# One ScalarE instruction per weight tile is tied to its place in the written order, and the stash tiles' decode starts six units after the load

## The chip, the cores and the metric

The kernel runs on one core of one Trainium2 chip, in one launch. The metric is device time in microseconds (us) from the first to the last instruction and what lies around them, as the median of several runs; less is better. The engines are TensorE (PE in the profile, its weight loads PEld), VectorE (DVE), ScalarE (ACT), GpSimd (POOL) and SyncE (SP), which issues every DMA of this kernel.

## The reference, cut to what matters

The weights arrive as 64-bit words on the device (where the host gives double precision), and the kernel turns each into float32 and then into a pair of float16, high and low; products of pairs are summed in float32. What is computed, for 8 batches of 576 tokens and 512 channels:

```python
kv = einsum('bhsd,bhse->bhde', k, v); o = einsum('bhsd,bhde->bhse', q, kv)
x = o / sqrt(mean(o*o, -1) + 1e-6) * g_norm          # heads side by side: 512 channels
theta = x @ w_theta
y = einsum('ts,bsd->btd', w_tok_r, x*cos(theta)) + einsum('ts,bsd->btd', w_tok_i, x*sin(theta))
u = x + y
x2 = u + relu(u @ w_ch)
u2 = x2 + (relu(x2.T @ w_tok1) @ w_tok2).T
out = u2 + relu(u2 @ w_ch1) @ w_ch2                  # 512 -> 1536 -> 512
```

## The kernel before

The kernel goes through the batches one after another, and then through eight large stages of the last two products (`mlp`), 64 us each. In the batch part each batch is made of small **units of work**, python generators with a `yield` between their steps. `go(unit)` first moves every pending unit on by one step and then starts the new one, so a step that stands behind n yields is written n units after the start of its own unit. The units of a batch from the third on, in this order: eight `mix` (27 matmuls each, into `py`), eight `channel` (12 matmuls, `pr`), `kv`, four `token1` (`ph`), `kv`, eight `token2` (`pu`); between them the next batch's five `attend` (`po`) and five `rotate` (`pt`) are put in. That makes 45 units with the five weight tiles below.

`spare()` puts units of weight preparation from the list `extra` in between. Beside the `channel` units of the first batch these are eleven tiles of `w_tok1` and `w_tok2` (`weight`: load, one yield, decode). From then on they are 24 tiles of `w_ch1` and `w_ch2` (`stash`, tiles `wa` and `wb` in the profile): each is loaded into `raw`, decoded, combined on GpSimd, split into `hi` and `lo`, and stored to device memory for `mlp`. Two stash tiles start in a batch's `widen_tokens` (behind its first and its fifth `token2`) and, from the third batch on, three more in its `mix` stage (behind `mix` 0, 2 and 5). The text calls the five that follow one another in this way S1 to S5. There are four batches with all five, then S1 and S2 alone once more; the batch ahead of them has two as well.

A stash tile has these steps: load on SP (L194 by way of L116); ScalarE's first decode step (L122); three VectorE steps (L124, L126, L127), the last two of which write into `raw`; four GpSimd instructions (L205 to L208) and ScalarE's L209; VectorE's L211; ScalarE's L213; VectorE's L215; two stores on SP (L218). `raw`, `hi`, `lo` and `t` have two buffers each. The other steps that matter: `mix` adds its sum to R on VectorE (L422), ScalarE writes `uh` (L423) and VectorE `ul` (L426); `channel` reads `uh` and `ul` on TensorE, and then runs L446 (VectorE), L447 (ScalarE), L453 (VectorE) and a transposing DMA into `xt` (L457), which `token1` waits for. `attend` goes through L298, L300 to L303, L308, L321, L323, a transposing DMA (L324), L327 and L329; `rotate` starts on ScalarE with L352. `kv` ends with ScalarE's L273.

Each engine executes its own queue in order. What that order is, the framework's scheduler decides when the program is built: of the instructions that it takes to be ready it issues the one written first, by its own estimate of when things finish. An instruction can therefore be queued far ahead of its written place when its engine has nothing else to do by that estimate. `tc.keep_in_program_order(x)` puts `x` behind the instruction of the same engine that was written just before it. Before the change it stands only at the loads (L116), for SP's queue.

Of the kernel before, what the change touches and what calls it, by code (L numbers as in the profile page):

```python
# [11 lines left out]
F32 = mybir.dt.float32  # L12
I32 = mybir.dt.int32
AF = mybir.ActivationFunctionType
# [14 lines left out]
def attn_mixer_kernel(  # L29
# [4 lines left out]
    nc = tc.nc  # L34
# [79 lines left out]
    def load(dst, src):  # L114

        tc.keep_in_program_order(nc.sync.dma_start(dst, src))  # L116

    def decode(val, raw, inplace=False):


        bits = val.bitcast(I32)
        nc.scalar.activation(val, raw[..., 1].bitcast(F32), AF.Copy, scale=2.0**-112)  # L122
        yield
        nc.vector.tensor_scalar(bits, bits, 3, None, ALU.logical_shift_left)  # L124
        to = raw[..., 0] if inplace else bits
        nc.vector.scalar_tensor_tensor(to, raw[..., 0], 29, bits, ALU.logical_shift_right, ALU.bitwise_or)  # L126
        nc.vector.scalar_tensor_tensor(to, raw[..., 1], -(2**31), to, ALU.bitwise_and, ALU.bitwise_or)  # L127

    def weight(pool, w, row, col, part, n, hi, lo, scale, name, raw=None):

        val = pool.tile([P, n], F32, tag="val", name=f"{name}v")[:part]
        rows = slice(row, row + part)
        if w.dtype == F32:
            load(val, w[rows, col:col + n])
            yield
        else:
            if raw is None:
                raw = pool.tile([P, n, 2], I32, tag="raw", name=f"{name}r")[:part]
                load(raw.rearrange("p n w -> p (n w)"), w.bitcast(I32)[rows, 2 * col:2 * (col + n)])
            yield  # L140
            yield from decode(val, raw)
        if w is not w_theta and w is not w_ch1:

            nc.scalar.activation(val, val, AF.Copy, scale=scale)
            nc.scalar.activation(hi, val, AF.Copy)
            yield
            nc.gpsimd.tensor_tensor(lo, val, hi, ALU.subtract)
            return
        nc.scalar.activation(hi, val, AF.Copy, scale=scale)
        yield  # L150
        nc.vector.scalar_tensor_tensor(lo, val, scale, hi, ALU.mult, ALU.subtract)
# [25 lines left out]
    wad = [dr.tile([P, KH, DH, 7, P], F16, name=f"wad{i}") for i in range(2)]  # L177
    wbd = [dr.tile([P, KH, MH, 7, P], F16, name=f"wbd{i}") for i in range(2)]

    wp = []  # L180

    def stash(w, name, rows, cols, dst):


        hi, lo = (wp[0].tile([P, 7, P], F16, tag=f"st{i}", name=f"{name}{i}") for i in range(2))

        words = () if w.dtype == F32 else (2,)
        raw = wp[0].tile([P, 4, P, *words], I32 if words else F32, tag="raw", name=f"{name}r")
        t = wp[0].tile([P, 4, P], F32, tag="val", name=f"{name}s")
        for half, at in ((0, slice(0, 4, 3)), (1, slice(1, 3))):  # L190
            src = (w.bitcast(I32) if words else w)[rows[half]:rows[half] + P, :]
            n = 2 if words else 1
            src = src.rearrange("p (a n) -> p a n", a=2)[:, :, n * cols:n * (cols + P)]
            load(raw[:, at].rearrange("p a n w -> p a (n w)") if words else raw[:, at], src)  # L194

        for _ in range(4):
            yield
        val = raw
        if words:

            yield from decode(t.rearrange("p x n -> p (x n)"), raw.rearrange("p x n w -> p (x n) w"), True)
            val = raw[..., 0].bitcast(F32)
        yield

        nc.gpsimd.tensor_tensor(t[:, 1], val[:, 3], val[:, 2], ALU.add)  # L205
        nc.gpsimd.tensor_tensor(t[:, 3], val[:, 3], val[:, 0], ALU.subtract)
        nc.gpsimd.tensor_tensor(t[:, 2], t[:, 1], val[:, 0], ALU.subtract)
        nc.gpsimd.tensor_tensor(t[:, 0], val[:, 1], t[:, 2], ALU.subtract)  # L208
        nc.scalar.activation(hi[:, :3], val[:, :3], AF.Copy, scale=SW)  # L209
        yield  # L210
        nc.vector.scalar_tensor_tensor(lo[:, :3], val[:, :3], SW, hi[:, :3], ALU.mult, ALU.subtract)  # L211
        yield
        nc.scalar.activation(hi[:, 3:], t, AF.Copy, scale=SW)  # L213
        yield
        nc.vector.scalar_tensor_tensor(lo[:, 3:], t, SW, hi[:, 3:], ALU.mult, ALU.subtract)  # L215
        yield
        for d, src in zip(dst, (hi, lo)):
            nc.sync.dma_start(d, src)  # L218

    def stash_wide(g, k):  # L220
        return stash(w_ch1, f"wa{g}{k}_", (k * P, (DH + k) * P), g * P, [t[:, g, k] for t in wad])

    def stash_narrow(g, m):
        return stash(w_ch2, f"wb{g}{m}_", (g * P, (KH + g) * P), m * P, [t[:, g, m] for t in wbd])
# [472 lines left out]
    tk, cp, first = [], [], iter(())  # L697
# [40 lines left out]
    for b in range(B):  # L738
# [49 lines left out]
        elif b + 2 == B:  # L788
# [11 lines left out]
            first = chunks(0)  # L800
# [59 lines left out]
```

## Time and profile before

| | us |
|---|---|
| median of 3 runs | 1177.6 (1174.95 to 1178.34) |
| the profiled execution | 1177.31 |
| its span, first to last instruction | 1175.5 |
| TensorE busy in the span | 1089.8 (93%) |
| VectorE busy | 849.6 (72%) |
| ScalarE busy | 562.5 (48%) |
| GpSimd busy | 236.3 (20%) |

The batch part takes the first 740 us, of which the stash tiles occupy 157 to about 560; `mlp` takes the rest. In the rows a time is in us from the start of the span; "idle before" is how long the engine stood still ahead of an instruction, and behind the arrow stands what ended that.

### The profile page before, as it was taken

The page shows a single profiled execution, that of the slowest core. Times are in us where ns is not written, and L with a number is a line of the kernel's source. Part 1 is how long each engine was busy: PE and PEld are TensorE (multiplying, and loading weights), DVE is VectorE, ACT ScalarE, POOL GpSimd, SP SyncE. Part 2 cuts the span into 40 slices and gives each one's busy share as a digit, 9 for nine tenths or more (in the row PEclk, how much of TensorE's full clock was granted, in tenths as well). Part 3 has the DMA queues.
Part 4 walks back from the last instruction along what each step waited for, and adds up shares of the span by engine and source line. Part 5 has one row for each costly group of instructions (what it writes and reads, how often), then busy time and mean ns, then how long its engine had stood idle before and what let it go on. Part 6 is the DMA issues. An engine that isn't in the chain of part 4 may idle for free.

```text
span 1175.5 us, 21915 instructions
## 1 busy us (share of the span) xinstructions
PE 1089.8 (93%) x8884; PEld 820.7 (70%) x8884; DVE 849.6 (72%) x1579; ACT 562.5 (48%) x1002; POOL 236.3 (20%) x258
## 2 busy tenths in 40 slices
PE   4759899898997997989999999999999999999998
PEld 3446666576665765767686777777777777777777
DVE  3997869798597696895955386857768584848583
ACT  2765645455264363462633163545536272626361
POOL 3774135072351450722400000000000000000000
PEclk9779999999998999999999999999999999999999
DMA  9616464592674666736273540101020202011101
GB/s 321 214 59 135 98 208 115 150 230 68 195 175 106 191 156 156 199 86 166 61 195 100 166 168 31 52 26 56 11 71 11 72 4 78 2 42 40 37 6 41
DMA packets 156357, 126.37 MB, mean 107 GB/s; under 512 B 93216, under 2 KB 137120, under 8 KB 156256
## 3 DMA queue, kind: packets, MB, share of 16 engines
q1 hardware_dynamic: 156256, 124.98, 38.0%
q8 instruction: 69, 1.13, 0.4%
q14 instruction: 32, 0.26, 0.1%
HBM read 74.29 MB, written 29.88 MB: 89 GB/s over the span
## 4 chain that ended last, share of the span: by engine, by line
PE 39%; DVE 36%; DMA 13%; ACT 4%; POOL 3%; issue 3%; SPq 2%; DVEq 0%; ACTq 0%; POOLq 0%
DMA xt<-xs 4%; PE na L82 3%; PE na L84 3%; PE na L83 3%; DVE gl L553 3%; DVE zl L367 3%; DVE gl L601 2%; DMA c<-u2d 2%; PE pa L82 2%; ACT gh L552 2%; PE pa L83 2%; PE pa L84 2%; PE pr L83 2%; DMA wa_r<-in_w_ch 1%; PE pr L84 1%
## 5 line engine op out<-in xcount | busy, mean ns | idle before, releaser
L82 PE MATMUL py<-wmh,zh 128*128 128x256 f16 (+1 forms) x576 | 166.8, 290 | 8.6 <-DMA zh<-zt 4.8
L83 PE MATMUL py<-wml,zh 128*128 128x256 f16 (+1 forms) x576 | 166.6, 290 | 0.0
L84 PE MATMUL py<-wmh,zl 128*128 128x320 f16 (+1 forms) x512 | 147.7, 289 | 5.3 <-DVE zl L367 5.3
L82 PE MATMUL na<-gh,wbh 128*128 128x288 f16 x384 | 106.7, 286 | 9.6 <-DVE c L612 9.6
L83 PE MATMUL pa<-o,wah 128*128 128x288 f16 x384 | 109.4, 286 | 0.0
L83 PE MATMUL na<-gl,wbh 128*128 128x288 f16 x384 | 109.1, 286 | 0.0
L84 PE MATMUL na<-gh,wbl 128*128 128x288 f16 x384 | 109.0, 286 | 0.0
L82 PE MATMUL pa<-o,wah 128*128 128x288 f16 x384 | 108.6, 286 | 0.2 <-DVE pre L595 0.2
L84 PE MATMUL pa<-o,wal 128*128 128x288 f16 x384 | 108.5, 286 | 0.0
L612 DVE SCALAR_TENSOR_TENSOR c<-na,c 128x288 f32<-128x288 f32 x64 | 28.5, 456 | 79.9 <-PE na L84 79.9
L82 PE MATMUL pr<-uh,wch 128*128 128x256 f16 (+1 forms) x256 | 76.3, 298 | 9.7 <-ACT uh L423 9.6
L83 PEld LDWEIGHTS <-wbh 128*128 128x128 f16 x672 | 65.7, 98 | 27.1 <-issue 10.7
L553 DVE TENSOR_TENSOR gl<-sum,gh 128x1152 f16<-128x1152 f32 x48 | 65.1, 1356 | 24.3 <-ACT gh L552 23.4
L83 PE MATMUL pr<-ul,wch 128*128 128x256 f16 (+1 forms) x256 | 76.2, 298 | 5.5 <-DVE ul L426 5.5
L83 PEld LDWEIGHTS <-wah 128*128 128x128 f16 x672 | 65.7, 98 | 17.7 <-issue 1.1
L82 PEld LDWEIGHTS <-wah 128*128 128x128 f16 x672 | 65.7, 98 | 16.6
L82 PEld LDWEIGHTS <-wbh 128*128 128x128 f16 x672 | 65.7, 98 | 16.6
L84 PEld LDWEIGHTS <-wbl 128*128 128x128 f16 x672 | 65.7, 98 | 16.6
L84 PEld LDWEIGHTS <-wal 128*128 128x128 f16 x672 | 65.7, 98 | 16.6
L84 PE MATMUL pr<-uh,wcl 128*128 128x256 f16 (+1 forms) x256 | 76.2, 298 | 0.0
L82 PEld LDWEIGHTS <-zh 128*128 128x128 f16 x576 | 57.1, 99 | 26.0 <-DMA zh<-zt 5.4
L302 POOL TENSOR_TENSOR ri<-ss,mhalf 128x8 f32<-128x8 f32 x40 | 71.4, 1785 | 2.0
(315 smaller groups left out, 2980.9 us busy)
## 6 DMA issues: line engine op xcount, KB each, us to landing
q<-in_q SPq DMA_DIRECT2D x8, 1152.0 KB, 7.2
c<-u2d SPq DMA_DIRECT2D x32, 288.0 KB, 4.4
out<-c SPq DMA_DIRECT2D x64, 144.0 KB, 1.8
k<-in_k SPq DMA_DIRECT2D x24, 256.0 KB, 4.8
v<-in_v SPq DMA_DIRECT2D x24, 256.0 KB, 5.1
wa_r<-in_w_ch SPq DMA_DIRECT2D x24, 256.0 KB, 3.9
wb_r<-in_w_ch SPq DMA_DIRECT2D x24, 256.0 KB, 3.8
wad<-wa SPq DMA_DIRECT2D x24, 224.0 KB, 2.1
```

The source lines that it names most:

```text
L82: nc.tensor.matmul(acc, ah, bh, start=first and i == 0, stop=False, **more)
L83: nc.tensor.matmul(acc, ah, bl, start=False, stop=False, **more)
L84: nc.tensor.matmul(acc, al, bh, start=False, stop=last and i == n - 1, **more)
L302: nc.gpsimd.tensor_tensor(ri, ss, mhalf, ALU.pow)
L367: nc.vector.tensor_tensor(zl[:, kk, :], t, zh[:, kk, :], ALU.subtract)
L552: nc.scalar.activation(h.hi[:, 3:], h.s, AF.Copy)
L553: nc.vector.tensor_tensor(h.lo[:, 3:], h.s, h.hi[:, 3:], ALU.subtract)
L601: nc.vector.tensor_tensor(h.lo[:, :3], h.own, h.hi[:, :3], ALU.subtract)
L612: nc.vector.scalar_tensor_tensor(dst, acc, 1.0 / SW**2, dst, ALU.mult, ALU.add)
```

## The change

The list `wp` is declared earlier, so that `decode` can ask whether the pool for the later weight tiles is open. If it is, ScalarE's first decode step is kept behind the ScalarE instruction written before it. That holds for the eleven tiles of `w_tok1` and `w_tok2` and for the 24 stash tiles; earlier tiles are untouched. In `stash` there are six yields in place of four between load and decode, so that all steps from the first decode step to the stores are written two units later. No operation is added or removed.

```diff
+    wp = []
+
     def decode(val, raw, inplace=False):
         bits = val.bitcast(I32)
-        nc.scalar.activation(val, raw[..., 1].bitcast(F32), AF.Copy, scale=2.0**-112)
+        first = nc.scalar.activation(val, raw[..., 1].bitcast(F32), AF.Copy, scale=2.0**-112)
+        if wp:
+            tc.keep_in_program_order(first)
         yield
...
-    wp = []
-
     def stash(w, name, rows, cols, dst):
...
-        for _ in range(4):
+        for _ in range(6):
             yield
```

## Rows read from the trace of the kernel before

**Rows 1.** The page, busy us, share of the span and instructions of each engine.
```profile
PE 1089.8 (93%) x8884; PEld 820.7 (70%) x8884; DVE 849.6 (72%) x1579; ACT 562.5 (48%) x1002; POOL 236.3 (20%) x258
```
**Rows 2.** Windows: us, PE, PEld, DVE, ACT, POOL busy (count), PEclk, DMA share, GB/s.
```profile
480.00:560.00 80.00, 74.61 (x632) 54.15 (x630) 65.88 (x127) 40.25 (x77) 30.98 (x38) 0.98 0.55 139
560.00:620.00 60.00, 59.88 (x483) 43.83 (x481) 43.27 (x89) 27.72 (x55) 10.82 (x12) 1.00 0.54 137
```
**Rows 3.** Waits of TensorE, 120 to 620 us: us in total, times, longest us.
```profile
PE pr L82 <- ACT uh L423: 9.6, 4, 2.5
PE ph L473 <- DMA xt<-xs: 6.5, 5, 1.9
...
PE pr L83 <- DVE ul L426: 5.5, 7, 1.1
...
PE pt L82 <- DMA xt<-xs: 0.3, 2, 0.2
```
**Rows 4.** Timeline of TensorE, 521.9 to 526.5 us: start, us, instruction [idle before <-releaser].
```profile
525.19 0.30 PE L82 MATMUL pr<-uh,wch 128*128 128x320 f16 x1 [2.54 <-ACT uh L423]
526.36 0.43 PE L83 MATMUL pr<-ul,wch 128*128 128x320 f16 x1 [0.87 <-DVE ul L426]
```
**Rows 5.** Timeline of VectorE, 500 to 541 us.
```profile
505.86 0.41 DVE L124 TENSOR_SCALAR wb_s<-wb_s 128x512 int32<-128x512 int32 x1
...
508.13 0.68 DVE L126 SCALAR_TENSOR_TENSOR wb_r<-wb_r,wb_s 128x512 int32<-128x512 int32 x1
...
511.74 0.95 DVE L127 SCALAR_TENSOR_TENSOR wb_r<-wb_r 128x512 int32<-128x512 int32 x1
...
516.47 0.55 DVE L211 SCALAR_TENSOR_TENSOR wb<-wb_r,wb 128x384 f16<-128x384 f32 x1
...
518.54 0.68 DVE L215 SCALAR_TENSOR_TENSOR wb<-wb_s,wb 128x512 f16<-128x512 f32 x1
...
524.15 0.48 DVE L422 TENSOR_TENSOR R<-py,R 128x320 f32<-128x320 f32 x1
...
534.92 0.56 DVE L453 SCALAR_TENSOR_TENSOR xs<-R,xs 128x256 f16<-128x256 f32 x2 [0.54 <-ACT xs L447]
```
**Rows 6.** Windows: a stretch of `mix`, and those just behind the four long pr waits.
```profile
491.60:528.70 37.10, 33.22 (x259) 22.31 (x258) 36.97 (x69) 25.04 (x49) 12.93 (x16) 0.96 0.43 114
...
526.00:529.40 3.40, 3.04 (x12) 1.77 (x12) 3.25 (x9) 1.70 (x5) 0.00 (x0) 0.50 0.30 56
sum 17.00, PE 14.41 PEld 8.05 DVE 15.89 ACT 8.67 POOL 0.00; mean PE 3.60 PEld 2.01 DVE 3.97 ACT 2.17 POOL 0.00
```
**Rows 7.** Timeline of ScalarE, 488 to 541 us.
```profile
497.50 0.63 ACT L327 ACTIVATE R<-xt 128x512 f32<-128x512 f16 x1
...
504.99 0.68 ACT L122 ACTIVATE wb_s<-wb_r 128x512 f32<-128x512 f32 x1 [0.33 <-DMA wb_r<-in_w_ch]
...
526.14 0.95 ACT L447 ACTIVATE xs<-R 128x256 f16<-128x256 f32 x2
```
**Rows 8.** Timeline of VectorE, two waits for ScalarE's first decode step.
```profile
330.57 1.16 DVE L124 TENSOR_SCALAR wa_s<-wa_s 128x512 int32<-128x512 int32 x1 [2.23 <-ACT wa_s L122]
...
478.75 0.43 DVE L124 TENSOR_SCALAR wb_s<-wb_s 128x512 int32<-128x512 int32 x1 [2.87 <-ACT wb_s L122]
```
**Rows 9.** Timelines of ScalarE and TensorE at the first token2 units.
```profile
161.63 0.66 ACT L122 ACTIVATE wa_s<-wa_r 128x512 f32<-128x512 f32 x1 [1.33 <-DMA wa_r<-in_w_ch]
...
163.47 0.28 PE L82 MATMUL pu<-w2h,hh 128*128 128x256 f16 x1 [1.63 <-ACT hh L75]
```
**Rows 10.** Timeline of SyncE, 452 to 500 us: start, us of issuing, DMA.
```profile
473.32 1.62 SPq L116 DMA_DIRECT2D wb_r<-in_w_ch  x2
475.03 0.60 SPq L218 DMA_DIRECT2D wbd<-wb  x1
```
**Rows 11.** Timelines of VectorE and GpSimd, an instruction of each side by side.
```profile
486.94 1.27 DVE L426 SCALAR_TENSOR_TENSOR ul<-R,uh 128x256 f16<-128x256 f32 x1
...
486.44 1.48 POOL L303 TENSOR_TENSOR x<-ri,gb 128x512 f32<-128x512 f32 x1
```

## The prediction

> **What bounds the kernel now.** I read the engines' busy times first: TensorE is busy for 93% of the span [rows 1], so only what makes TensorE wait, or slows its clock, can be gained. By stages, it has no wait to speak of once the stash tiles are over (59.88 of 60 us) and does wait while they run (74.61 of 80) [rows 2]. Next the list of TensorE's waits for 120 to 620 us [rows 3]. The largest are those of `pr`, the `channel` products, for `uh` and `ul`: 9.6 + 5.5 = 15.1 us. They come in four bundles, one in each of the four batches with five stash tiles, 3.8 us each on average; the timeline of the fourth shows the main part, 2.54 and 0.87 us [rows 4].
>
> Then the question is who is late there. `uh` and `ul` hang on VectorE's L422 of the last `mix`, which runs at 524.15 [rows 5], while TensorE already stood waiting. VectorE is busy for 36.97 of the 37.10 us up to 528.7 [rows 6]: it is a backlog, not a latency. Five of the instructions in that backlog are S5's: L124, L126, L127, L211 and L215, at 505.86 to 518.54, 0.41 + 0.68 + 0.95 + 0.55 + 0.68 = 3.27 us [rows 5]; with L127 at the 0.68 of L126, which has the same size, 3.0. I take 3.1. So the stretch that sets the end is VectorE's work from S2's decode to the last `mix`, and ScalarE's long waits for stash loads matter only where VectorE then stands still with other work behind it.
>
> The clock hangs on the same waits: behind each bundle there is a stretch at half the granted clock, 1.2 of 2.4 GHz (0.50 in the windows); together TensorE is busy 14.41 us in them [rows 6], which would be 7.2 at full clock. So the four bundles cost 15.1 + 7.2 = 22.3 us.
>
> **The change, part by part.** Nothing is added, so what counts is where each pinned instruction can now go. I counted the units to find the ScalarE instruction written just before each first decode step.
>
> *S5, the term that carries the forecast.* With six yields S5's L122 is written right behind L447 of the batch's first `channel` unit. That L447 runs at 526.14, S5's L122 at 504.99 [rows 7]. L447 comes after L422 of the last `mix` on VectorE, so all five of S5's VectorE instructions leave the backlog in front of it: 4 x 3.1 = **-12.4 us** of 15.1. The lower bound is the whole 15.1, the upper bound 0, if by then VectorE is no longer backlogged; I take nearly all, because the backlog is 3.8 deep and only 3.1 goes.
>
> *S3 and S4* are written behind L327 of an `attend` (497.50 in the fourth batch) [rows 7] and behind L352 of a `rotate`, so they move some 10 us later but stay ahead of the last `mix`: VectorE's sum there is the same. What goes is a wait of 2.23 us in the second of the four batches [rows 8], of which only the 0.7 counts that S5 leaves of that bundle: **-0.7**. Against it, VectorE could run dry in the middle, where work is now missing: 0 to 1.5 us a batch, of which I take none, the backlog being dense.
>
> *S1* goes behind `kv`'s L273, that is behind the `hh` copies and no longer in front of them. In steady state TensorE hardly waits for these copies, so this earns nothing. At the first `token2` units it does: L122 holds ScalarE for 1.33 us and TensorE waits 1.63 for the copy behind it [rows 9]; half of that, **-0.8** (bounds 0 and -1.6).
>
> *S2* goes behind S1's L213, which was ahead of it anyway. Its load stays at 473.32 on SP [rows 10] and the wait of 2.87 us that it causes on VectorE [rows 8] stays; bounds -3 and +2 a batch (S1's two units more), taken at 0.
>
> *The tiles of `w_tok1` and `w_tok2`* stand behind instructions that already run ahead of them: 0, bounds -1 and +1.
>
> *What follows behind the last `mix`.* S5's five VectorE instructions, four on GpSimd, two on ScalarE and two stores on SP now fall into the `channel` stage and the `kv` and `token1` units behind it. There VectorE idles 0.54 us in each unit [rows 5], and then while TensorE does `kv` and `token1`, so it has room; but the chain from the last `pr` through L446, L447, L453 and the transpose to `ph` is already exposed, 6.5 us in five waits [rows 3]. One instruction of 0.68 in front of that chain each time: 4 x 0.7 = **+2.8** (bounds 0 and 4 x 3.1 = 12.4, all five in front). SP: the stores are written between the third and the fourth pair's transposes; they wait for L213 and L215, and hold the last transpose if those are late. That is inside the same bounds.
>
> *Clock.* With 0.7 us of wait left of 3.8 I expect three of four half-clock stretches to go: 7.2 x 3/4 = **-5.4** (bounds 0 and -7.2).
>
> The sum: -12.4 - 0.7 - 0.8 + 2.8 - 5.4 = -16.5, from the profiled execution's 1177.31 (span 1175.5 and 1.8 around it): 1160.8. The median of the runs is 0.3 higher: 1161.1. The best bounds together give -15.1 - 7.2 - 1.6 = -23.9, or 1153.
>
> **A rule that speaks against it.** While GpSimd's L303 ran from 486.44 to 487.92, a VectorE instruction of 256 columns took 1.27 us [rows 11], though those of 512 columns take 0.68 [rows 5]: at least 0.6 lost to the neighbour. The Trainium skill, SBUF — State Buffer, section SBUF: two separate sides, says why: GpSimd and a VectorE instruction with two SBUF inputs take turns at one pair of ports, and the later one is blocked for the other's whole instruction. By it, S5's GpSimd work moves from a crowded stretch, where it already cost VectorE something, into the `channel` stage, where GpSimd is idle now.
>
> **Rivals.**
> *The tail takes S5's VectorE work back.* All five go in front of the last chain to `ph`: +12.4 in place of +2.8, so 1171. For it: they are written earlier than the later `channel` units, so once ready they go first. Against it: VectorE's L211 and L215 wait on ScalarE, and the 0.54 us gaps take most of the rest.
> *The tail takes it back and GpSimd blocks VectorE there too.* Four GpSimd instructions at 0.6 us are 2.4 more a batch: 3.1 + 2.4 - 0.7 = 4.8 a batch over the forecast, 19.2 in all: 1180, no change. That is the rule above taken to its end; the rows show single blocks of this size, not four in a row.
> *The change doesn't do what it says.* A pin reaches only one instruction back; if the scheduler already places that predecessor early, S5 stays in front of the last `mix`: 1177. Against it: L447 hangs on `pr`, which TensorE does after all of `mix` but the last sums.
> *Slower: S2's load falls behind S1's stores.* On SP, S2's load (473.32) stands ahead of S1's second store (475.03) by 1.7 us [rows 10]. S1's steps now come two units later; 45 units take the 80 us or so between one batch's bundle of `pr` waits and the next, 1.8 each, so 3.6 us. If the queue puts both stores in front of the load, it starts at 475.0 + 3.6 + 0.6 = 479.2, 5.9 us later, and S2's decode with it, with ScalarE and VectorE standing behind it. That is 5.9 of new idle time on the backlogged VectorE against 3.1 gained: 4 x 2.8 = +11, 1188. It decides from 3.1 us of growth on. The queued `attend` steps behind it feed `pt`, which already has waits (0.3 us in two, so no slack at some) [rows 3]. Against it: in the written order S2's load stands ahead of S1's stores, and both stores are ready later than the load.
>
> **How the numbers follow.** Forecast (1153 to 1168) 0.55; tail takes it back, 1171, 0.12; with GpSimd, 1180, 0.08; no effect, 1177, 0.09; slower, 1188, 0.16. A measurement of this kernel can tell about 0.3%, 3.5 us, from no change. Faster: 0.55 + 0.12 = 0.67; same: 0.08 + 0.09 = 0.17; slower 0.16. The range leaves out the slower case and a little at the bottom: 1153 to 1180.
>
> **What would show it.** Right: S5's L122 behind L447; the `pr` waits of 15.1 us down to 2 to 4; the half-clock stretches behind them gone; `ph` waits up by less than 3 us in all. Wrong: `ph` waits grown by 10 us (tail), VectorE's wait before S2's L124 grown beyond 6 us and new `pt` waits (slower), S5's L124 still ahead of the last `mix`'s L422 (no effect).

## The result and the profile after

The changed kernel takes 1194.0 us (median; 1191.4 to 1194.8) against 1177.5 of the kernel before, measured beside it: ratio 1.014, with an interval of 1.0118 to 1.0163. The profiled execution has a span of 1191.6 us, 16.1 over that of before. The forecast was 16 us faster, and the time lies 14 us above the range.

The page, busy us of each engine (after):

```profile
PE 1095.6 (92%) x8884; PEld 823.4 (69%) x8884; DVE 847.9 (71%) x1579; ACT 558.5 (47%) x1002; POOL 238.1 (20%) x258
```

TensorE does the same instructions as before [rows 1] in 5.8 us more. That is the clock: it is busy at half clock for 63.0 us against 52.4, and the 10.6 more would be 5.3 at full clock. The other 10.3 of the 16.1 us are idle time. The list of TensorE's waits, 120 to 620 us (us in total, times, longest), after:

```profile
PE kvp L271 <- DMA v<-in_v: 14.9, 7, 3.7
PE pr L82 <- ACT uh L426: 10.0, 4, 3.6
PE ph L476 <- DMA xt<-xs: 8.2, 10, 1.6
PE pt L82 <- DMA xt<-xs: 5.9, 5, 2.0
...
PE pr L83 <- DVE ul L429: 1.9, 4, 0.5
PE pt L82 <- DVE wa L218: 1.2, 1, 1.2
```

The same list of before beyond [rows 3]:

```profile
PE kvp L268 <- DMA v<-in_v: 5.6, 5, 2.1
```

The `pr` waits, which were to fall from 15.1 us to 2 to 4, are at 11.9. New are 9.3 us for `kvp`, 6.8 for `pt` (0.3 before) and 1.7 for `ph`. Two of the new waits are followed by stretches at half clock of 6.70 us, as long as the longest behind a `pr` wait of before. Windows (us, PE, PEld, DVE, ACT, POOL, granted clock, DMA share, GB/s), first that one of before, then two of after:

```profile
365.60:372.40 6.80, 5.22 (x20) 2.84 (x20) 6.11 (x17) 3.13 (x8) 0.00 (x0) 0.50 0.41 76
467.20:473.90 6.70, 5.76 (x14) 2.04 (x15) 0.69 (x1) 0.60 (x1) 0.00 (x0) 0.50 0.87 267
552.50:559.20 6.70, 5.55 (x15) 2.01 (x15) 0.69 (x1) 0.60 (x1) 0.00 (x0) 0.50 0.43 123
```

VectorE is all but idle in the two of after: TensorE does the `kv` and `token1` products there, and what it waits for is not VectorE at that moment but a load or a transpose that was sent late.

S5's first step did go where the forecast put it. ScalarE's timeline of after, fourth batch:

```profile
536.90 0.40 ACT L450 ACTIVATE xs<-R 128x256 f16<-128x256 f32 x1
537.21 0.65 ACT L124 ACTIVATE wb_s<-wb_r 128x512 f32<-128x512 f32 x1
```

(L450 is L447 of before and L124 is L122. In the changed kernel decode's three VectorE steps, L124, L126 and L127 before, are L129, L131 and L132, and the later lines lie three lower. In the kernels with one group pinned these three are the same and the later lines lie four lower: L211 and L215 of before are L215 and L219, L446 and L453 are L450 and L457.)

To see in which stage the time went, I took from TensorE's timeline the first `pu`, the first `pr` and the first `ph` product of each batch and cut the time of the four batches with five stash tiles there: **mix** is first `pu` to first `pr` of the next batch (`token2` and `mix` alternate), **channel** is first `pr` to first `ph`, **token1** is first `ph` to first `pu` (`token1` and `kv`). Sums over the four batches, in us, for this pair and for most of the kernels below:

| kernel | mix | channel | token1 | total | against before |
|---|---|---|---|---|---|
| before | 195.1 | 76.1 | 44.7 | 315.9 | |
| after | 203.3 | 73.6 | 56.5 | 333.4 | +17.5 |
| after, four units | 205.5 | 74.5 | 42.7 | 322.7 | +6.8 |
| before, six units | 195.7 | 75.1 | 44.0 | 314.8 | -1.1 |
| S5 pinned alone, six units | 195.3 | 69.4 | 52.5 | 317.2 | +1.3 |
| S3, S4 pinned alone, six | 194.5 | 87.2 | 42.7 | 324.4 | +8.5 |
| S1, S2 pinned alone, six | 203.6 | 71.0 | 44.3 | 318.9 | +3.0 |
| before, S5 out | 195.6 | 66.7 | 46.1 | 308.4 | -7.5 |
| after, S5 out | 200.1 | 75.7 | 43.0 | 318.8 | +2.9 |
| after, q late | 201.8 | 63.3 | 47.9 | 313.0 | -2.9 |
| before, q late | 195.1 | 75.7 | 41.1 | 311.9 | -4.0 |
| after, S5's stores late | 202.8 | 75.0 | 54.7 | 332.5 | +16.6 |
| after, S5 at fourteen | 196.2 | 75.8 | 46.0 | 318.0 | +2.1 |
| after, S5 at fourteen, q late | 195.4 | 71.1 | 53.6 | 320.1 | +4.2 |
| S5 pinned alone, fourteen | 194.7 | 66.8 | 48.6 | 310.1 | -5.8 |

Each row is one execution, and the times of one kernel's executions spread over 3 to 11 us, so a few us between two totals say little by themselves.

So the loss is 8.2 us in mix and 11.8 in token1, and the gain looked for in channel is 2.5. What the `w_tok` tiles and the first `token2` units gain ahead of the four batches can't be read from this pair: the first `ph` of the second batch is at 212.0 against 214.5, but three kernels that change nothing up to there (S5 alone at six and at fourteen units, and before with S5 out) have it at 212.1, 215.9 and 215.0.

### The profile page after: what moved, and what is told of

Same layout as the page of the kernel before. It is cut to its first block, busy times and chain, and to the rows that moved or that the text cites. A ratio compares the mean times of both kernels' runs of the same rounds, so it can differ in the third digit from the quotient of the medians.

```text
span 1191.6 us, 21923 instructions
## 1 busy us (share of the span) xinstructions
PE 1095.6 (92%) x8884; PEld 823.4 (69%) x8884; DVE 847.9 (71%) x1579; ACT 558.5 (47%) x1002; POOL 238.1 (20%) x258
## 4 chain that ended last, share of the span: by engine, by line
PE 35%; DVE 35%; DMA 14%; ACT 6%; POOL 5%; issue 3%; SPq 1%; POOLq 0%; ACTq 0%; DVEq 0%
DMA xt<-xs 6%; PE na L82 3%; PE na L84 3%; PE na L83 3%; DVE gl L556 3%; DVE gl L604 2%; DVE zl L370 2%; DMA c<-u2d 2%; PE pa L82 2%; ACT gh L555 2%; PE pa L83 2%; PE pa L84 2%; PE py L84 2%; PE py L82 1%; PE py L83 1%
## 5 line engine op out<-in xcount | busy, mean ns | idle before, releaser
L83 PEld LDWEIGHTS <-wbh 128*128 128x128 f16 x672 | 65.7, 98 | 26.8 <-issue 10.3
L82 PEld LDWEIGHTS <-wah 128*128 128x128 f16 x672 | 65.8, 98 | 16.6
L82 PEld LDWEIGHTS <-wbh 128*128 128x128 f16 x672 | 65.7, 98 | 16.6
L84 PEld LDWEIGHTS <-wal 128*128 128x128 f16 x672 | 65.7, 98 | 16.6
L84 PEld LDWEIGHTS <-wbl 128*128 128x128 f16 x672 | 65.7, 98 | 16.6
```

Of the source, the lines that this page charges most:

```text
L82: nc.tensor.matmul(acc, ah, bh, start=first and i == 0, stop=False, **more)
L83: nc.tensor.matmul(acc, ah, bl, start=False, stop=False, **more)
L84: nc.tensor.matmul(acc, al, bh, start=False, stop=last and i == n - 1, **more)
```

## The experiments

Each time is compared with runs of the kernel before that were made beside it, since their median moved by up to 3 us (1174.6 to 1177.5); ratios with their intervals.

**The two halves of the change.** The pins with four units:

```diff
-        for _ in range(6):
+        for _ in range(4):
             yield
```

> The pin alone, with the four yields of before. Theory A: the loss has two parts, about +12 us in the kv/token1 stages of the four batches with five stash tiles, because S5's VectorE steps and stores now lie among the channel units, and about +8 in the mix stages, because S3 and S4 now stand behind an attend and a rotate step and VectorE waits for them. With four yields S5 stands behind a rotate step and ahead of the channel units' L447, so the first part should go and the second stay: 1180 to 1186. Theory B: the whole loss is from the pins reordering the mix stage (late transposes, pt waits): 1190 to 1196 as with the change.

Measured: 1184.2 us, 1.0072 (1.0052 to 1.0093). A: token1 is back at 42.7, and mix stays long at 205.5. The other half, six units and no pin (`range(6)` in the kernel before):

> Six yields and no pin. A and B alike: the scheduler still places the first step as soon as it takes the load to have landed, so the order on ScalarE is that of before and the time too: 1175 to 1180. If the two units alone carry the loss: about 1190.

Measured: 1178.0 us, 1.0013 (0.9998 to 1.0028). The two units by themselves move nothing: without the pin ScalarE takes the step as early as before. The loss belongs to the pins, and grows with S5's later place.

**S5 later.** In the changed kernel, and then in the kernel before with no other tile pinned (`S5` in the diffs holds the four tiles wa30_, wa51_, wb20_ and wb41_):

```diff
-        for _ in range(6):
+        for _ in range(14 if name in S5 else 6):
             yield
```

> The changed kernel, but S5 waits 14 units in place of 6 between load and first step, so that all its steps fall behind the batch's last channel unit, where VectorE is idle for some 8 us. Theory A: the kv/token1 stages are back to what they were before, -11 to -13 us against the changed kernel, and the bundle of pr waits stays as it is: 1181 to 1184. Theory B: no gain: 1191 to 1196.

Measured: 1181.4 us, 1.0038 (1.0025 to 1.0051). A: token1 is at 46.0, and the `pr` waits are not shorter (16.5 us). S5 alone, against the changed kernel (`pin` is true for the tiles in `S5`):

```diff
-        if wp:
+        if pin:
             tc.keep_in_program_order(first)
...
-        for _ in range(6):
+        for _ in range(14 if name in S5 else 4):
             yield
```

> The kernel before, but S5 alone is pinned and waits 14 units; S1 to S4 and the tok tiles as before. Theory A: S5's 3.1 us leave VectorE's backlog in front of the last mix and fall into an idle stretch: the pr waits (15.1 us) drop to 3 to 5 and with them half-clock stretches, 1160 to 1168, faster than both kernels. If the pr waits do not hang on VectorE's backlog: 1175 to 1180.

Measured: 1172.0 us, 0.9966 (0.995 to 0.9981), the lowest ratio of all, though between the two ranges that were expected. TensorE's waits of this kernel:

```profile
PE kvp L272 <- DMA v<-in_v: 7.5, 4, 2.5
PE ph L477 <- DMA xt<-xs: 5.9, 7, 1.6
PE pr L82 <- ACT uh L427: 4.4, 4, 2.1
...
PE ph L477 <- DVE R L450: 3.4, 1, 3.4
...
PE pr L83 <- DVE ul L430: 1.7, 4, 0.5
```

The `pr` waits fall by 9.0 us, and 4.7 of it comes back at `ph` and `kvp`. With S4 as late as S5, and the w_tok tiles pinned:

> S4 and S5 pinned and late by 14 units, the tok tiles pinned, S1 to S3 and q as before. If the pr waits hang on VectorE's backlog (6.1 us left with S5 alone gone), another 3 us a batch takes them to 1.5 us or less and the half-clock stretches with them: 1162 to 1167. If the held raw buffers stop SP in front of the next k and v loads: kvp waits grow and it is 1170 or more.

Measured: 1182.5 us, 1.0045 (1.0023 to 1.0067). The `pr` waits are down to 0.9, but `kvp` is at 19.7 and `ph` at 16.0: 14.2 us leave the stretch ahead of `pr`, and 23.6 come back behind it. The time and the `kvp` waits are as the second case of the expectation has them; whether held `raw` buffers are the reason was not tried.

**The parts of the pin one by one.** The same edit as in the last diff with six units, for S5 alone, for S3 and S4 alone, and for S1 and S2 alone. First S5, which is the forecast's main step by itself:

> The kernel before with S5 alone pinned and at six yields (its first step right behind the ScalarE step of the batch's first channel unit, as in the changed kernel); S1 to S4 and the w_tok tiles as before. It is the forecast's main step by itself. A (the forecast: 12.4 us less of pr waits, 5.4 of half clock, 2.8 more in the tail): 1160 to 1165, pr waits 2 to 4 of 15.1. B (S5's steps between the channel units take most of it back there, ph and kvp waits 8 to 12 us higher): 1170 to 1175, pr waits 2 to 6.

Measured: 1177.4 us, 1.0021 (1.0007 to 1.0034), above B's range too, with B's waits. They are:

```profile
PE ph L477 <- DMA xt<-xs: 14.4, 8, 2.8
PE kvp L272 <- DMA v<-in_v: 8.8, 5, 3.3
...
PE ph L477 <- DVE R L450: 3.2, 1, 3.2
PE pr L82 <- ACT uh L427: 2.8, 4, 1.3
...
PE pr L83 <- DVE ul L430: 1.6, 4, 0.5
```

The `pr` waits do what was forecast: 4.4 of 15.1, 10.7 less. `ph` has 11.1 more and `kvp` 3.2 more. VectorE's timeline of this kernel, fourth batch, shows why (the last `pr` product ends at 526.50):

```profile
521.94 0.42 DVE L457 SCALAR_TENSOR_TENSOR xs<-R,xs 128x256 f16<-128x256 f32 x1 [0.15 <-ACT xs L451]
522.50 0.43 DVE L129 TENSOR_SCALAR wb_s<-wb_s 128x512 int32<-128x512 int32 x1
522.85 0.42 DVE L457 SCALAR_TENSOR_TENSOR xs<-R,xs 128x256 f16<-128x256 f32 x1
523.18 0.68 DVE L131 SCALAR_TENSOR_TENSOR wb_r<-wb_r,wb_s 128x512 int32<-128x512 int32 x1
523.79 0.41 DVE L450 SCALAR_TENSOR_TENSOR R<-pr,R 128x256 f32<-128x256 f32 x1
524.12 0.68 DVE L132 SCALAR_TENSOR_TENSOR wb_r<-wb_r 128x512 int32<-128x512 int32 x1
...
525.05 0.68 DVE L457 SCALAR_TENSOR_TENSOR xs<-R,xs 128x256 f16<-128x256 f32 x1
525.65 0.86 DVE L215 SCALAR_TENSOR_TENSOR wb<-wb_r,wb 128x384 f16<-128x384 f32 x1
526.44 0.68 DVE L457 SCALAR_TENSOR_TENSOR xs<-R,xs 128x256 f16<-128x256 f32 x1
...
528.93 0.68 DVE L219 SCALAR_TENSOR_TENSOR wb<-wb_s,wb 128x512 f16<-128x512 f32 x1
...
532.55 0.56 DVE L457 SCALAR_TENSOR_TENSOR xs<-R,xs 128x256 f16<-128x256 f32 x2 [0.54 <-ACT xs L451]
```

Among the units' own L450 and L457 stand all five steps of S5. The fifth, L219, fills one of the gaps of 0.54 us and costs nothing, as the forecast had it for nearly all. The other four come while VectorE still has the end of the `mix` work and the first units in front of it. The last L457 ends 6.6 us behind the last `pr` product; before it was 2.3 (the last L453 of [rows 5] ends at 535.48, the last `pr` at 533.16). The last transpose, the k and v loads behind it and with them `ph` and `kvp` come later by as much. The gaps that are left at the end don't make it good: they are the time from L450 through ScalarE's L451 to L457, one in a unit of 1.5 us (from L457 at 531.05 to L457 at 532.55), whatever the lateness.

S3 and S4 alone:

> The kernel before with S3 and S4 alone pinned and at six yields; S1, S2, S5 and the w_tok tiles as before. A (the places of S3 and S4 by themselves make VectorE stand in the mix stage, for GpSimd's sums ahead of L218 and for attend 2's late transpose, 1.5 to 3.5 us a batch): VectorE's idle time in the four mix stages 11 to 20 us against 5.4, 1182 to 1190. B (they cost only together with S5's place): idle as before within 3 us, 1174 to 1179.

Measured: 1185.5 us, 1.009 (1.0072 to 1.0108), A by its time. Its waits:

```profile
PE pr L82 <- ACT uh L427: 12.2, 4, 3.5
PE pr L83 <- DVE ul L430: 11.1, 8, 1.8
```

The `pr` waits are 23.3 us against 15.1. But VectorE's idle time in the four mix stages is 6.6 us against 5.4, not 11 to 20, so A's mechanism isn't it. What the trace shows instead is that the stash steps crowd to the end: before, the last of S5's five VectorE steps runs 5.6 us ahead of the last `mix` sum (L215 at 518.54 and L422 at 524.15 [rows 5]); here the fourth of them runs at 528.20, right in front of that sum (529.47), and the fifth behind it. Over the four batches the last sum comes 6.5 us later behind the first `mix` product. From 6 us behind that product to the sum VectorE is busy for 2.7 us more in all, with about as many instructions (296 against 297), so they are stretched, and it stands still for 3.0 us more in larger and smaller gaps. Why S3's and S4's places do this stays open.

S1 and S2 alone (with them the two pairs that stand without S3 to S5):

> The kernel before with S1 and S2 alone pinned and at six yields (and the two pairs that stand alone); S3, S4, S5 and the w_tok tiles as before. S3 and S4 alone cost 8.6 us over the four batches, S5 alone 1.3, all together 17.6. A (S1 and S2 are what puts S2's VectorE steps in front of attend 0's, whose transpose then goes 1 to 2 us later, so that pt waits 0.7 to 2 us in three batches): mix of the four batches 199 us or more against 195.1, pt waits 3 to 5 us, 1179 to 1184. B (attend 0 is late only because S3, S4 and S5 move too): mix 195 to 196, pt waits under 1 us, 1175 to 1178.

Measured: 1180.2 us, 1.0054 (1.0029 to 1.0078). A: mix is 203.6 us, 8.5 more, and the changed kernel has 8.2 more. Its `pt` waits:

```profile
PE pt L82 <- DMA xt<-xs: 7.2, 6, 2.0
```

VectorE's timeline at that place, third batch, before:

```profile
400.72 0.84 DVE L124 TENSOR_SCALAR wb_s<-wb_s 128x512 int32<-128x512 int32 x1 [3.25 <-ACT wb_s L122]
401.48 0.68 DVE L308 TENSOR_TENSOR x<-po,x 128x512 f32<-128x512 f32 x1
402.08 0.68 DVE L126 SCALAR_TENSOR_TENSOR wb_r<-wb_r,wb_s 128x512 int32<-128x512 int32 x1
```

and after (L311 is L308 of before):

```profile
403.42 0.43 DVE L129 TENSOR_SCALAR wb_s<-wb_s 128x512 int32<-128x512 int32 x1 [3.33 <-ACT wb_s L124]
403.88 0.69 DVE L131 SCALAR_TENSOR_TENSOR wb_r<-wb_r,wb_s 128x512 int32<-128x512 int32 x1
404.49 0.42 DVE L425 TENSOR_TENSOR R<-py,R 128x256 f32<-128x256 f32 x1
404.82 0.68 DVE L132 SCALAR_TENSOR_TENSOR wb_r<-wb_r 128x512 int32<-128x512 int32 x1
405.42 0.69 DVE L311 TENSOR_TENSOR x<-po,x 128x512 f32<-128x512 f32 x1
```

What pays for it, on TensorE:

```profile
412.28 0.49 PE L82 MATMUL pt<-wth,xt 128*128 128x512 f16 x1 [2.02 <-DMA xt<-xs]
```

Both stand behind the same wait of 3.3 us for S2's load. Before, the `attend` step ran second; now it runs fifth, behind three steps of S2. Its transpose leaves 10.5 us behind the first `mix` product instead of 8.4, and `rotate` waits 2.02 us for it. In the other batches the waits there are 0.5, 1.2 and 0.8.

**No S5 in the stretch.** Four tiles a batch, the four left over in the next batch's `mix`:

```diff
-            if b == 0 or b > 1 and i in (0, 2, 5):
+            if b == 0 or b > 1 and i in ((0, 2) if b < 6 else (0, 2, 5, 7)):
                 spare()
```

> The kernel before with four stash tiles in a batch in place of five: no tile starts behind mix 5 of the four batches, and the four that are left over start in the mix stage of the batch behind them (four there, where none stood). A (S5's VectorE work is the backlog that makes the pr waits, and in the channel stage it costs): pr waits of 15.1 us down to 3 to 7 (one bundle may come in the extra batch), channel to pu of the four batches not longer than before (44.7 us), 1157 to 1166. B (the backlog stays, other work fills the place): pr waits over 10, 1170 to 1178.

Measured: 1178.7 us, 1.003 (1.0014 to 1.0046), above both ranges. The `pr` waits of the four batches fall to 6.0 us, as A has it; the batch behind them has 3.7. The four batches are 7.5 us shorter, but the batch that takes the four tiles has a channel stage of 30.5 us in place of 23.5, and all is gone again. Even with S5 out of the way for nothing, the four batches give 7.5 us, where the forecast counted 12.4 + 5.4 for it: with `pr` on time, TensorE goes through channel faster, and the last L453 ends 3.0 to 5.6 us behind the last `pr` instead of 1.6 to 2.5.

> The changed kernel with the same four tiles a batch. No S5 stands in the tail, and S1 to S4 and the w_tok tiles are pinned, at six yields. A (the pins of S1 to S4 have a price of their own in the mix stage, some 5 to 8 us over the four batches: attend 0 behind S2's steps, VectorE waiting for GpSimd and for the transpose behind q): 1168 to 1175, mix of the four batches 199 us or more against 195.1. B (without S5 in the tail the pins cost nothing): 1157 to 1166, mix 195 to 197.

Measured: 1182.5 us, 1.0063 (1.0041 to 1.0085), above both ranges, with the mix of A (200.1). The pins on S1 to S4 have a price of their own: 10.4 us over the four batches against the last kernel, 4.5 of it in mix. And the `pr` waits are 14.4 us, with no S5 in the stretch at all.

**The q load.** In the changed kernel `attend` 2's transpose is issued right behind the load of q. SyncE's timeline of after, fourth batch:

```profile
497.31 0.67 SPq L257 DMA_DIRECT2D q<-in_q  x1
498.03 0.72 SPq L259 DMA_DIRECT2D q<-in_q  x1
500.73 1.26 SPq L327 DMA_TRANSPOSE xt<-xs  x1
```

The DMA issues of that stretch (KB each, us from issue to landing):

```profile
q<-in_q SPq DMA_DIRECT2D x1, 1152.0 KB, 9.0
...
xt<-xs SPq DMA_TRANSPOSE x1, 8.5
```

What waits for that transpose on ScalarE:

```profile
509.22 0.63 ACT L330 ACTIVATE R<-xt 128x512 f32<-128x512 f16 x1 [4.71 <-DMA xt<-xs]
```

And behind it VectorE, with a second wait in the same stretch:

```profile
509.88 0.69 DVE L332 SCALAR_TENSOR_TENSOR R<-xt,R 128x512 f32<-128x512 f16 x1 [4.00 <-ACT R L330]
...
519.70 0.69 DVE L218 SCALAR_TENSOR_TENSOR wb<-wb_s,wb 128x512 f16<-128x512 f32 x1 [1.55 <-ACT wb L216]
```

VectorE's idle time in the four mix stages of the changed kernel (gaps over 0.25 us, from 6 us behind the first `mix` product to the last) is 19.7 us against 5.4. 7.1 of it are waits for L330 at the transposes behind q, and 6.2 are the wait of 1.55 us ahead of L218, once in each batch: ScalarE's L216 stands there for GpSimd. This idle time lies in the backlog, so it takes the place of S5's 12.4. The test is to write the q loads behind the last `mix` (with `load`, so SyncE issues them in that place):

```diff
+    def load_q(o):
+        qs = qT[o.b].rearrange("h p s -> p h s")
+        load(o.q[:, :, :S], qs)
+        load(o.q[:, :, S:], qs[:, :, SM:])
...
-                after = load_heads(b + 2)
+                after = load_heads(b + 2, True)
...
+        if after is not None:
+            load_q(after)
```

> The changed kernel, with the load of q for the batch after next issued behind the batch's last mix in place of behind its fourth, so that no transposing DMA of attend is issued while q is in flight. Theory A': the mix part of the loss is DMA: the third transpose was issued 2.4 to 3.6 us behind q and landed after 5.1 to 8.5 us. It should land in 3 to 4, the pt waits (7.1 us) fall to 1 or less, and the time to 1184 to 1188; the kv/token1 part stays. Theory B', the mix part is the stash steps themselves on ScalarE and VectorE (S3 and S4 waiting for GpSimd): 1191 to 1195.

Measured: 1176.9 us, 1.001 (0.999 to 1.0031): in time the whole loss is gone, more than A' expected, but not where A' looked for it. Mix keeps 6.7 of the 8.2 us that it had grown by, and the `pt` waits stay at 5.8; channel is 10.3 us shorter than in the changed kernel and token1 8.6. The transpose lands in 3.1, 3.1, 3.1 and 4.8 us (5.1, 5.2, 5.9 and 8.5 in the changed kernel; 4.6, 3.1, 3.3 and 3.6 before), VectorE's idle time in mix is 8.1, and the waits are:

```profile
PE ph L483 <- DMA xt<-xs: 15.6, 9, 3.2
PE kvp L278 <- DMA v<-in_v: 8.0, 5, 3.5
PE pt L82 <- DMA xt<-xs: 5.8, 5, 2.7
...
PE pr L82 <- ACT uh L433: 0.8, 1, 0.8
```

`pr` is free, and as with S5 alone `ph` has 9 us more. VectorE's waits ahead of L218 go too, so the order on the engines has changed as well as the landing: the run shows that q's place decides, not that the landing alone does. The same edit in the kernel before:

> The kernel before with one edit: the two q loads of the batch after next are written behind the batch's last mix unit, nothing pinned, four yields. It tells whether the 17 us that the same edit gave back in the changed kernel belong to the change. A (q's load costs only where attend 2's transpose is issued within about 4 us behind it, which the change brought about): in the kernel before the four transposes landed in 4.6, 3.1, 3.3 and 3.6 us, 2.2 us in all above the undisturbed 3.1, so 1174 to 1178, the four landing in 3.1 each. B (a later q load is a gain of its own, whatever the order of the stash steps): 17 us less, 1158 to 1165.

Measured: 1173.7 us, 0.9992 (0.9981 to 1.0003), where the kernel before has 1174.8: no gain of its own, A. With S5 at fourteen units in the changed kernel:

> The changed kernel with S5 at fourteen units (1181.4 so far) and the two q loads written behind the last mix. A (what q costs is the lateness of attend 2's transpose: 6.0, 3.2, 4.0, 5.5 us to landing in the four batches, 6.3 above 3.1 in all): 1174 to 1177, the transposes landing in 3.1 to 4. B (the 17 us of the same edit beside S5's early place are a fixed amount): 1162 to 1167. pr waits of 16.5 us fall to 10 or less by A.

Measured: 1179.9 us, 1.0038 (1.0025 to 1.0051), where it was without q's move; neither A nor B. The transposes land in 3.0 to 3.9 us, channel falls by 4.7 us, and token1 grows by 7.6. With the pins at four units:

> The pin with four yields and the late q. There the third transpose was issued 0.7 to 1.5 us behind q and landed after 6.8 to 10.8 us, with 9.0 us of pt waits. Theory A': 1174 to 1178, no slower than the kernel before. Theory B': 1182 to 1186.

Measured: 1178.5 us, 1.0016 (0.9994 to 1.0037), nearer to A. With S5 alone at fourteen and the w_tok tiles pinned:

> S5 alone pinned and late as in the run of S5 alone (1172), with the pin at the eleven tok tiles and the late q as well. The tok pins gave 2.5 us up to the first token1 in the changed kernel; q costs little here, as the third transpose is 5 us behind it: 1167 to 1171.

Measured: 1173.9 us, 0.9981 (0.9961 to 1.0), above the expected range and no better than S5 alone at fourteen.

**S5's stores.** The two stores wait at the head of SyncE's queue, ahead of the last transposes and of the k and v loads. With them kept ten units later, and every other order that of the changed kernel:

```diff
+        for _ in range(10 if name in S5 else 0):
+            yield
         for d, src in zip(dst, (hi, lo)):
-            nc.sync.dma_start(d, src)
+            st = nc.sync.dma_start(d, src)
+            if name in S5:
+                tc.keep_in_program_order(st)
```

> The changed kernel with S5's two stores alone kept ten units later on SyncE, behind the last transposes of channel and the next k and v loads; every engine's order is otherwise that of the changed kernel. A (the stores, waiting for S5's last VectorE step at the head of SyncE's queue, hold the transposes, the k and v loads and the next stash load behind them by 1 to 2 us): kvp waits of 14.9 us down to 6 to 10, ph waits 8.2 down to 5 to 7, 1184 to 1189. B (the tail's lateness is VectorE's and ScalarE's, the stores only pass it on): kvp and ph waits as before within 2 us, 1191 to 1195.

Measured: 1193.7 us, 1.0166 (1.0143 to 1.0189). B: token1 is 1.8 us shorter and the time is that of the changed kernel. With q late as well:

> Both edits in the changed kernel: the q loads behind the last mix, and S5's two stores ten units later. With q late alone the time was 1176.9 with pr waits of 1.0 us, ph 15.6, kvp 8.0. A (the stores at the head of SyncE's queue make a good part of the ph and kvp waits): ph down to 8 to 12, kvp to 3 to 6, 1167 to 1172. B (VectorE and ScalarE make them): 1175 to 1178, waits as they were.

Measured: 1178.0 us, 1.0024 (1.0004 to 1.0044), B again. By these two runs the stores pass the lateness on and don't make it.

## Why the prediction was wrong

Term by term, forecast and measured in the changed kernel, in us: `pr` waits -13.1 and -3.2; the tail (`ph` and `kvp`) +2.8 and +11.0; the `pt` waits 0 and +6.8; the clock -5.4 and +5.8; the `pu` waits -0.8 and -2.3.

**S5's step, -12.4: right, but not a gain.** The step went behind L447, and where it moves alone the `pr` waits fall by 10.7 us. What failed is that the stretch that sets the end was taken to run "from S2's decode to the last `mix`". With S5 alone the end hangs on VectorE up to the last L453 of channel (L457 there), and S5's steps stayed in front of that. A step moved from ahead of one wait to ahead of the next moves the wait.

**The tail, +2.8 with bounds 0 and +12.4: the upper end.** With S5 alone it is 11.1 us at `ph` and 3.2 more at `kvp`, which the bounds left out. The reason given, that VectorE idles 0.54 us in each unit and "so it has room", is the step that failed: four of the five steps come before there is such a gap, and the gap is the latency of a loop through ScalarE of 1.5 us a unit, in which lateness is not made good. The rival "the tail takes it back" had the mechanism, and against it was held this same sentence.

**"Of which I take none, the backlog being dense": wrong.** The 0 to 1.5 us a batch for VectorE running dry came out at 3.6 in the changed kernel (19.7 against 5.4 us), 1.8 of it at transposes behind q and 1.55 behind GpSimd. That q's load is on the same queue just ahead of the shifted transposes was not looked at: the forecast followed what the moved steps themselves issue, and not what the steps behind them now come next to. S3 and S4 were priced at -0.7 and cost 8.5 by themselves.

**S2, taken at 0 with bounds -3 and +2 a batch: the upper end.** Mix grew by 8.5 us with S1 and S2 alone; the two were not tried apart. The rival that came out slower put it on S2's load falling behind S1's stores; the load did not move against the products around it (VectorE's wait for it is 3.33 us in place of 3.25). It is the order of VectorE's queue behind that load which changed. The sign of that rival was right, and its cause wrong.

**The clock, -5.4: the other sign.** It follows the waits. From 120 to 680 us TensorE is granted half clock in 11 stretches of 47.8 us together, against 9 of 34.1, and its busy time grows by 5.8. Of the 13.7, 3.4 stand at 218 us, where S5 alone, with nothing changed up to there, has them too, so that much need not come from the change.

**S1 at the first `token2`, -0.8:** right in kind; the waits of `pu` fell from 3.2 us to 0.9, and to 0.4 with S1 and S2 alone.

**GpSimd's blocking,** the rule of the Trainium skill (SBUF — State Buffer, section SBUF: two separate sides), is there in the tail, but small. With S5 alone, beside GpSimd's four instructions, three VectorE steps in a batch are longer: L215 takes 0.86 us in place of 0.55 (L211 in [rows 5]) and two L457 take 0.68 each in place of 0.42. That is 0.8 us a batch and not 2.4.

**The best bounds together, 1153,** leave out the -3 a batch of S2 and the -1 of the `w_tok` tiles that the prediction names. The miss is on the other side, so nothing hangs on it.

The three groups of pins alone make +1.3, +8.5 and +3.0 us in the table, 12.8 of 17.5 together. By their medians, each against the kernel before beside it, they make +1.6, +9.8 and +5.6, which is 17.0 where the changed kernel has 16.6: in time they add up as far as this can tell. By stages they don't: token1 is 56.5 us, where the three changes add up to 50.1. Two things stay open: how the pins on S3 and S4, the largest part, make the last sum late, and why the whole loss goes when q's load is moved although mix keeps its share.

## What to carry to other kernels

When an engine is behind, follow its queue past the first wait that it causes, to where it is next owed something: work taken out ahead of one wait is a gain only if it lands behind the last of them, or where the engine is truly free. An idle gap that returns in every unit between two engines that answer each other is latency: a step that fits into it may cost nothing, as L219 here, but lateness from before is not made good there. And where an order is pinned, look at what else moves: a big load that a small transfer now follows, and the steps of other units that are now queued behind the pinned one.

## What the runs showed of the hardware

At the shortest a transpose to `xt` lands 3.1 us after its issue (before and after, for instance the first one of `attend` in the fourth batch's mix stage). Issued 2.7 to 3.0 us behind the second part of the q load, whose parts of 1152 and 128 KB take 6.4 to 9.9 us, it landed in 5.1 to 8.5 us (after), and issued 0.7 to 1.2 us behind it in 6.8 to 10.8 (pins with four units). In all eight cases it landed 0.9 to 2.4 us behind that part's own landing. I had not expected a small transfer to be held for as long as that.
